# Attention and a gated feed-forward layer on one core: the first layer of eight chunks as seven Strassen products per pair of chunks, with streamed weight variants

## Chip, core and metric

The program runs on one core of one Trainium2 chip. The time is that of one execution on the device, in microseconds (us). Engines are named as in the profile: PE (TensorE, matmuls), PEld (its weight loads), DVE (VectorE), ACT (ScalarE), POOL (GpSimd) and SP (SyncE, which issues the DMAs here). Each engine works through its own list of instructions in order; semaphores make it wait for others.

## What is computed

```python
def _attn_ref(q, k, v, w_phi):                 # 8 batches, 8 heads, 576 tokens, 64 features
    def phi(x):
        proj = np.einsum('bhsd,df->bhsf', x, w_phi)
        proj = proj - np.max(np.abs(proj), axis=-1, keepdims=True)
        return np.concatenate([np.exp(proj), np.exp(-proj)], axis=-1)
    q_p, k_p = (phi(q), phi(k))
    kv = np.einsum('bhsf,bhsd->bhfd', k_p, v)
    z = np.sum(k_p, axis=2)
    num = np.einsum('bhsf,bhfd->bhsd', q_p, kv)
    den = np.einsum('bhsf,bhf->bhs', q_p, z)[..., None] + 1e-06
    return num / den
def _moe_ref(x, w_gate, w_val, w_out):         # x: 4608 tokens x 512, d_ff 1536
    g = x @ w_gate
    silu = g * (1.0 / (1.0 + np.exp(-g)))
    return silu * (x @ w_val) @ w_out
```

The attention's output, with the heads side by side, is the x of the second part. All of it is fp32; the weights come as 64-bit floats.

## The kernel before

**Tiles.** Attention works on 32 pairs of heads (pair i is batch i // 4, heads 2(i % 4) and the next). The feed-forward part works on twelve chunks of 384 tokens (`CH`), numbered 0 to 11 in the code, and on twelve slices f of 128 of the 1536 hidden features. The title's chunks 5 to 12 are 4 to 11 in the code.

**Split operands.** Most matmuls are made three times: each fp32 operand is split in a rounded high part (fp32r, by an ACT copy) and the rest (low, by a subtraction), and the product is hi*hi + hi*lo + lo*hi. All go through the helper `matmuls` (L274). So `first` (the gate and the value, `gv`) has 2 x 4 x 3 = 24 matmuls of 384 columns for a chunk and an f, and `second` (the second layer, into the banks `o`) nine of 512 columns. The high weights stay in SBUF (`w1_hi`, `w2_hi`); the low ones are stored in DRAM (`wlo_dram`) and loaded again for each chunk and f (`low_parts`, L618), 512 KB for the first layer and 256 KB for the second.

**Attention.** The first 8 pairs (`EARLY_PAIRS`) use plain fp32 matmuls and turn Q's projection with TensorE (L460); the other 24 split their operands and use VectorE's transposes. A pair projects K in five slots of 128 tokens (the last two overlap), takes the largest magnitude, makes both exponentials, sums `kv` and z in one matmul per slot, head and sign (20 of 128 columns, L411, with 64 columns of ones for z), projects Q, and makes numerators and denominators. The late pairs' exponentials are split by ACT (`qh`) and VectorE (`ql`, L534). The result is rounded and split into `xh`, `xl`, three sets of them, so attention can run at most that far ahead.

**Weights.** `weight_piece` turns 512 64-bit numbers per partition to fp32: a load, one ACT step, seven VectorE steps (L297 to L312), one ACT rounding, a store of the low part. There are 36 pieces, three for each f.

**Order.** The program is written as a list of steps with dependences, ranks and costs (`Plan`), and a list scheduler writes each engine's instructions in the order in which they could start by these costs. TensorE takes attention first (rank i) and feed-forward products behind it (rank 1000 and on); ACT, VectorE and SP take feed-forward steps first (`FIRST`). Chunks 0 to 2 run f by f while weights arrive (with 1 and 2 kept in `h_dram` for a second layer later); 3 to 11 follow one by one.

Of the kernel before, what the change touches and what calls it, by code (L numbers as in the profile page):

```python
# [17 lines left out]
P = 128  # L18
S = 576
# [25 lines left out]

# [11 lines left out]
class Plan:  # L57
# [3 lines left out]
    LAG = {"PE": 220, "ACT": 90, "DVE": 90, "SP": 2000}  # L61
# [120 lines left out]
def favor_attention_moe(ctx: ExitStack, tc: tile.TileContext, qT, kT, v, w_phi, wg, wv, wo, out):  # L182
# [7 lines left out]
    h_dram = tc.dram_tile([EARLY, NFT, P, CH], F32, name="h_dram")  # L190
# [56 lines left out]
    ps_kv = bank("kv")  # L247
    work = [bank(f"work{i}") for i in range(2)]
# [3 lines left out]
    wbd, wst = sb("wbd", [P, 2 * NF]), osb[1][:, :NF]  # L252
# [4 lines left out]
    for hi, lo, w in ((wbd_hi, wbd_lo, wbd), (wst_hi, wst_lo, wst)):  # L257
        nc.scalar.copy(hi, w)
        nc.vector.tensor_tensor(out=lo, in0=w, in1=hi, op=ALU.subtract)
    for h in range(2):  # L260
        nc.gpsimd.memset(vf[0][:, :, h, (1 - h) * D:(2 - h) * D], 1.0)
# [15 lines left out]
    weights_done = []  # L277
    w_ready, lo_stored, raw_free, wa_free = {}, {}, [None] * len(raw), [None] * len(wa)
    we_free = [None] * len(we)

    def weight_piece(f, a, rank):
# [10 lines left out]
        lo = w1_lo[f % LO_SETS][:, a].rearrange("p k f -> p (k f)") if a < 2 else w2_lo[f % LO_SETS]  # L292
# [16 lines left out]
        s6 = add("DVE", dve(n), lambda: vec.tensor_tensor(out=x, in0=x, in1=e, op=ALU.add), [s5], rank)  # L309
        we_free[u % len(we)] = s6  # L310
        s7 = add("ACT", act(n), lambda: nc.scalar.copy(hi, x), [s6], rank)
        s8 = add("DVE", dve(n), lambda: vec.tensor_tensor(out=lo, in0=x, in1=hi, op=ALU.subtract),  # L312
                 [s7, *(lo_user[a // 2][f - LO_SETS] if f >= LO_SETS else ())], rank)
# [8 lines left out]
    lo_user = ([], [])  # L322

# [4 lines left out]
    x_ready = {}  # L328
    early_done = []
# [3 lines left out]
    def attention(i, rank):  # L333
        b, pr = divmod(i, NPAIR)
        plan.early = early = i < EARLY_PAIRS
# [9 lines left out]
        k_in = add("SP", P * S * 4, lambda: nc.sync.dma_start(kin[j], kT[b, pr]), [last.get(("kin", i - 1))], rank)  # L345
# [11 lines left out]
        if early:  # L357
            k_ready = [k_in]
        else:
            k_hi = add("ACT", act(S), lambda: nc.scalar.copy(k_parts()[:, 0], kin[j]),  # L360
# [115 lines left out]
        else:  # L476
# [26 lines left out]
            def largest():  # L503
                vec.tensor_reduce(out=qm, in_=blocks(qe[j]), axis=AX.X, op=ALU.max, apply_absolute_value=True)
# [300 lines left out]
```

## Time and profile before

| What | Value |
|---|---|
| Timed runs, median of three (range) | 1305.03 us (1304.68 to 1305.92) |
| Span of the profiled execution, first to last instruction | 1304.0 us |
| Mean granted TensorE clock | 0.997 |
| First-layer matmuls (`gv`), 3456 of 384 columns, pieces of the chain | 45.3% of the span |
| Second-layer matmuls, 1296 of 512 columns (with others into the `o` banks) | 24.3% |
| `kv` matmuls of attention (L411) | 11.0% |
| Moved by DMA | 168.13 MB, mean 129 GB/s |

The profiled execution is one of the program; its time on the device beyond the span is not given, and the runs' median lies 1.0 us above the span. A group's row reads: line, engine, operation, output <- inputs, shapes, count | busy us, mean ns of one | idle time of the engine before them and what ended it. In the timeline a row has start, length, engine, line and operation, and x counts merged instructions.

### The profile page before, as it was taken

How to read it: one execution, taken by the hardware profiler on the slowest of the kernel's cores; microseconds unless marked ns; L12 is line 12 of the kernel's file. 1: busy time of each engine (PE TensorE's matmuls, PEld its weight loads, DVE VectorE, ACT ScalarE, POOL GpSimd, SP SyncE). 2: the span in 40 equal slices, each digit the busy share in tenths (PEclk: the TensorE clock that was granted, in tenths of full speed). 3: DMA queues.
4: the chain of work that ended last, by engine and by line, in shares of the span. 5: the costliest groups of instructions: out<-in, count | busy, mean ns of one | idle time of the engine just before them, and what ended most of it. 6: DMA issues, size and time to landing. Idle time of an engine off the chain costs nothing.

```text
span 1304.0 us, 19612 instructions
## 1 busy us (share of the span) xinstructions
PE 1281.7 (98%) x7554; PEld 1204.5 (92%) x7554; DVE 876.0 (67%) x1529; ACT 646.3 (50%) x1255; POOL 1.6 (0%) x9
## 2 busy tenths in 40 slices
PE   7999899999999999999999999999999999999998
PEld 6998899999778999999999999999999999999997
DVE  6997899997788767852777878732387786322222
ACT  5777433336676666631656665631365675221211
POOL 0000000000000000000000000000000000000000
PEclk9999999999999999999999999999999999999999
DMA  4343355553564443444443344354343443354443
GB/s 132 102 133 95 105 168 188 173 170 113 181 182 127 126 125 102 125 125 125 142 120 108 101 125 122 103 156 131 104 145 105 119 121 96 117 152 121 146 125 101
DMA packets 105564, 168.13 MB, mean 129 GB/s; under 512 B 46336, under 2 KB 52736, under 8 KB 105472
## 3 DMA queue, kind: packets, MB, share of 16 engines
q1 hardware_dynamic: 105152, 166.76, 43.1%
q8 instruction: 59, 0.97, 0.3%
q14 instruction: 33, 0.27, 0.1%
q10 hardware_dynamic: 320, 0.13, 0.0%
HBM read 143.26 MB, written 23.59 MB: 128 GB/s over the span
## 4 chain that ended last, share of the span: by engine, by line
PE 94%; DVE 2%; DMA 2%; ACT 1%; issue 1%; ACTq 0%; SPq 0%; DVEq 0%
PE gv L274 45%; PE o L274 24%; PE work L274 12%; PE kv L411 11%; DMA out_dram<-osb 1%; DMA w_lo<-wlo_dram 1%; PE o L460 1%; ACT osb L700 0%; DVE hl L677 0%; DVE km L387 0%; DVE qs L482 0%; DMA wbd<-in_w_phi_dram 0%; DVE kp L392 0%; DVE ql L534 0%; PE gv L751 0%
## 5 line engine op out<-in xcount | busy, mean ns | idle before, releaser
L274 PE MATMUL gv<-xh,w_hi 128*128 128x384 f32 x1152 | 389.4, 338 | 1.2 <-DVE th L653 1.2
L274 PE MATMUL gv<-xh,w_lo 128*128 128x384 f32 x1152 | 387.3, 336 | 0.0
L274 PE MATMUL gv<-xl,w_hi 128*128 128x384 f32 x1152 | 386.6, 336 | 0.0
L274 PEld LDWEIGHTS gv<-xh,w_hi 128*128 128x128 f32 x1152 | 216.7, 188 | 6.9 <-DVE th L653 1.9
L274 PEld LDWEIGHTS gv<-xl,w_hi 128*128 128x128 f32 x1152 | 216.7, 188 | 4.8
L274 PEld LDWEIGHTS gv<-xh,w_lo 128*128 128x128 f32 x1152 | 216.5, 188 | 0.0
L651 ACT ACTIVATE th<-gv 128x384 f32<-128x384 f32 x144 | 70.8, 492 | 265.8 <-PE gv L274 262.6
L653 DVE SCALAR_TENSOR_TENSOR th<-th,gv 128x384 f32<-128x384 f32 x144 | 78.9, 548 | 154.0 <-ACT th L651 153.5
L274 PE MATMUL o<-w_lo,hh 128*128 128x512 f32 x432 | 172.3, 399 | 1.0 <-DMA w_lo<-wlo_dram 0.8
L274 PE MATMUL o<-w_hi,hh 128*128 128x512 f32 x432 | 171.3, 396 | 2.0 <-ACT osb L700 1.8
L274 PE MATMUL o<-w_hi,hl 128*128 128x512 f32 x432 | 171.2, 396 | 0.0
L411 PE MATMUL kv<-vf,kp 128*128 128x128 f32 x1280 | 156.5, 275 | 0.0
L411 PEld LDWEIGHTS kv<-vf,kp 128*128 128x128 f32 x1280 | 153.0, 192 | 2.2 <-ACT kp L399 0.2
L676 ACT CAST hh<-th 128x384 fp32r<-128x384 f32 x144 | 73.7, 511 | 163.8 <-DVE th L656 148.6
L656 DVE TENSOR_TENSOR th<-th,gv 128x384 f32<-128x384 f32 x144 | 79.4, 551 | 67.2 <-PE gv L274 64.5
L399 ACT ACTIVATE kp<-kp 128x512 f32<-128x512 f32 (+1 forms) x192 | 105.8, 557 | 24.5 <-DVE kp L392 22.0
L568 DVE STREAM_TRANSPOSE qe<-den 128x576 f32<-128x576 f32 x32 | 24.9, 777 | 128.6 <-ACT den L561 128.6
L677 DVE TENSOR_TENSOR hl<-th,hh 128x384 fp32r<-128x384 f32 x144 | 79.2, 550 | 34.1 <-ACT hh L676 33.6
L274 PEld LDWEIGHTS o<-w_hi,hl 128*128 128x128 f32 x432 | 81.6, 189 | 19.1
L274 PEld LDWEIGHTS o<-w_lo,hh 128*128 128x128 f32 x432 | 81.5, 189 | 15.9 <-DMA w_lo<-wlo_dram 3.5
L274 PEld LDWEIGHTS o<-w_hi,hh 128*128 128x128 f32 x432 | 81.5, 189 | 15.3 <-ACT osb L700 2.6
L559 ACT COPY num<-work 64x288 f32<-64x288 f32 x103 | 40.5, 393 | 53.3 <-PE work L274 52.4
(103 smaller groups left out, 1762.7 us busy)
## 6 DMA issues: line engine op xcount, KB each, us to landing
w_lo<-wlo_dram SPq DMA_DIRECT2D x108, 512.0 KB, 3.6
w_lo<-wlo_dram SPq DMA_DIRECT2D x132, 256.0 KB, 3.1
kin<-in_kT_dram SPq DMA_DIRECT2D x32, 288.0 KB, 3.2
qin<-in_qT_dram SPq DMA_DIRECT2D x32, 288.0 KB, 2.9
wlo_dram<-w_lo SPq DMA_DIRECT2D x36, 256.0 KB, 2.3
out_dram<-osb SPq DMA_DIRECT2D x36, 256.0 KB, 3.2
vf<-in_v_dram SPq DMA_DIRECT2D x64, 128.0 KB, 3.1
shared<-in_wg_dram SPq DMA_DIRECT2D x12, 512.0 KB, 3.7
```

What stands on the lines that cost most here:

```text
L274: nc.tensor.matmul(o, l, r, start=a, stop=z)
L399: nc.scalar.activation(o, x, AF.Exp, scale=-1.0 if s else 1.0)
L411: nc.tensor.matmul(o, kp[buf][:, t - t0, h, s], vf[j][:, t, h], start=t == 0 and h + s == 0, stop=t == 4 and h + s == 2)
L460: nc.tensor.transpose(o[:, (h * w + t) * P:(h * w + t + 1) * P], y[:, 2 * t + h], ident)
L559: copied.append(add("ACT", act(SH), lambda key=key, ra=ra, c=c: nc.scalar.copy(num[ra, c], work[plan.bank[key]][ra, :SH]), [nu, free], rank))
L568: t0 = add("DVE", dve(S), lambda: vec.transpose(turned, den), [*copied, *done], rank)
L651: s1 = add("ACT", act(CH), lambda: nc.scalar.activation(t_, ps_gv[0][:, :CH], AF.Tanh, scale=0.5), [ends[0], th_free[j]], FIRST)
L653: s2 = add("DVE", dve(CH), lambda: nc.vector.scalar_tensor_tensor(out=t_, in0=t_, scalar=1.0, in1=ps_gv[0][:, :CH], op0=ALU.add, op1=ALU.m ...
L656: s3 = add("DVE", dve(CH), lambda: nc.vector.tensor_tensor(out=t_, in0=t_, in1=ps_gv[1][:, :CH], op=ALU.mult), [s2, ends[1]], FIRST)
L676: s4 = add("ACT", act(CH), lambda: nc.scalar.copy(hh[b], th[j]), [made, hid_free[b]], FIRST)
L677: s5 = add("DVE", dve(CH), lambda: nc.vector.tensor_tensor(out=hl[b], in0=th[j], in1=hh[b], op=ALU.subtract), [s4], FIRST)
```

## The change

**Products.** Chunks 4 to 11 are taken two at a time (c and c + 1). Their activations are split in two halves of the 512 input features, and gate and value play the two columns of a 2 x 2 block product. Strassen's form (Winograd's additions) makes it with seven products of 256 input features in place of eight. `operands` builds seven activation operands (three of them read as they are, four by four subtractions of VectorE) and splits each: seven ACT roundings and seven VectorE subtractions of 768 columns. `strassen` has, for each f, seven products of six matmuls (L965), three ACT copies out of a bank that goes on accumulating, three VectorE additions, two tanh and four multiplications behind them, of which the last is on GpSimd (L1036). Chunk c's second layer is done in three pieces (`piece`) among the products of the next f, with its `hl` by GpSimd; chunk c + 1's hidden values go to `h_dram`, and its second layer follows (`rest`).

**Weights.** Two of a piece's seven VectorE steps go to GpSimd (L332, L335). Three of the seven variants of the weights are copied from the raw high and low parts; four are sums, made by `sums` from a fp32 copy in DRAM (`w32_dram`) with GpSimd and one ACT rounding. All lie in `wv_dram`, and `strassen` streams each (256 KB) through a ring of twelve slots, which the second layer's low weights share. The high first-layer weights' place is then taken by the operands.

**Attention.** Twelve pairs are early instead of eight. K's last slot holds the last 64 tokens of both heads in one 128-column projection; `kv` has 16 matmuls of 65 columns and two of 130. `kv` takes a bank from the same three as the projections, and the products keep one of the three from chunk 4 on. The late `ql` are made by GpSimd. From chunk 3 on the output goes to DRAM (`x_dram`, L680) and is loaded again (`bring` for chunk 3, `operands` for the rest).

```diff
+EARLY_PAIRS = 12
+BANK_PAIRS = 8
+PLAIN = 4
+N_VAR = 7
...
-        s6 = add("DVE", dve(n), lambda: vec.tensor_tensor(out=x, in0=x, in1=e, op=ALU.add), [s5], rank)
+        s6 = add("POOL", pool2(n), lambda: nc.gpsimd.tensor_tensor(out=x, in0=x, in1=e, op=ALU.add), [s5], rank)
...
-        s8 = add("DVE", dve(n), lambda: vec.tensor_tensor(out=lo, in0=x, in1=hi, op=ALU.subtract),
-                 [s7, *(lo_user[a // 2][f - LO_SETS] if f >= LO_SETS else ())], rank)
+        s8 = add("POOL", pool2(n), lambda: nc.gpsimd.tensor_tensor(out=lo, in0=x, in1=hi, op=ALU.subtract),
+                 [s7, *(lo_user[a // 2][f - LOW_SETS[a // 2]] if f >= LOW_SETS[a // 2] else ()), *lo_copied.get(f - LO_SETS, ())], rank)
...
+        if a < 2:
+            wa_free[u % len(wa)] = stash[f, a] = add("SP", P * n * 4, lambda: nc.sync.dma_start(
+                w32_dram[f, :, a * DM:(a + 1) * DM], x), [s6, s8], rank)
...
+                        if both:
+                            nc.tensor.matmul(ps_kv()[:, s * 2 * VD:(s + 1) * 2 * VD], kp[buf][:, 0, 0, s],
+                                             vl.rearrange("p h d -> p (h d)"), start=False, stop=s == 1)
...
-                done += [g0, add("DVE", dve(2 * S), lambda k=k, part=part: vec.tensor_tensor(
+                done += [g0, add("POOL", pool2(2 * S), lambda k=k, part=part: nc.gpsimd.tensor_tensor(
                     out=flat(ql[k]), in0=flat(part), in1=flat(qh[k]), op=ALU.subtract), [g0, f1], rank)]
...
+            if c >= EARLY:
+                lo = add("SP", P * width * 4, lambda c=c, at=at, src=src, width=width: nc.sync.dma_start(
+                    x_dram[c - EARLY, :, pr, at:at + width], src), [t3], rank)
...
+    def stream(src, ready):
+        n = stream_n[0]
+        stream_n[0] += 1
+        stream_users[n] = []
+        older = stream_users[n - len(SLOTS_OF)] if n >= len(SLOTS_OF) else x_free[PLAIN - 1]
+        return n, add("SP", P * DM * 4, lambda: nc.sync.dma_start(stream_view(n).bitcast(F32), src),
+                      [*ready, *older], FIRST)
...
+        for f in range(NFT):
+            a, cc = gv(f, 0), gv(f, 1)
+            j1, s1 = unit
+            p2 = prod(f, 1, cc, True, [gv_read[(f + 1) % 2]])
+            g1 = plus(j1, cc, [s1, p2])
+            gv_read[(f + 1) % 2] = g1
+            t1, tg1 = gate(j1, g1)
+            p5 = prod(f, 4, zb, True, [third["free"]])
+            p6 = prod(f, 5, a, False, [s1])
+            j2, s2 = copy_out(a, [p6])
+            if f + 1 < NFT:
+                unit = begin_unit(f + 1)
+            else:
+                piece(0)
+            p7 = prod(f, 6, a, False, [s2])
+            j3, s3 = copy_out(a, [p7])
+            v2 = plus(j3, zb, [s3, p5])
...
+            p4 = prod(f, 3, a, False, [s3])
...
+            p3 = prod(f, 2, zb, False, [v2])
+            g2 = plus(j2, zb, [s2, p3])
...
-    for c in range(EARLY, NCH):
-        attend((c + 1) * CH)
-        for f in range(NFT):
-            j, h = first(c, f, low_parts(f, 0))
-            put_off(c, f, parts(j, h), low_parts(f, 1))
...
+    for c in range(PLAIN, NCH, 2):
+        attend((c + 2) * CH)
+        t = operands(c)
+        left = strassen(c, t, third, list(waiting))
+        waiting[:] = left
+        rest(c + 1)
```

**Where the instructions stand.** TensorE in the last chunks, before: `first` for one f, the gate's bank filled from end to end by twelve matmuls, then the value's (`xh`, `xl` the activations, `w1_hi`, `w1_lo` the weights).

```order
L274 MATMUL gv0_143<-xh2_99,w1_hi4_73 128x384
L274 MATMUL gv0_143<-xl2_102,w1_hi4_73 128x384
L274 MATMUL gv0_143<-xh2_99,w1_lo0_93 128x384
L274 MATMUL gv0_143<-xh2_99,w1_hi4_73 128x384
L274 MATMUL gv0_143<-xl2_102,w1_hi4_73 128x384
L274 MATMUL gv0_143<-xh2_99,w1_lo0_93 128x384
```

TensorE now, in the last pair of chunks, from p4 of one f to p7 of the next (`tb` the operands and some stream slots, `stream` the other slots, `work1` the third bank).

```order
L965 MATMUL gv0_139<-tb1_4439,tb3_4414 128x384 x6
L965 MATMUL work1_142<-tb1_4439,tb3_4414 128x384 x6
L296 MATMUL o2_138<-w2_hi7_83,hh1_127 128x512
L296 MATMUL o2_138<-stream_xl0_4396,hh1_127 128x512
L296 MATMUL o2_138<-w2_hi7_83,hl1_129 128x512
L965 MATMUL gv0_139<-tb0_4394,stream_xh0_4390 128x384 x6
L965 MATMUL work1_142<-tb2_4436,stream_xh0_4390 128x384 x6
L965 MATMUL gv1_140<-tb2_4436,stream_xl0_4396 128x384 x6
L965 MATMUL gv0_139<-tb0_4394,stream_xl0_4396 128x384 x6
L965 MATMUL gv1_140<-tb3_4414,stream_xl0_4396 128x384 x6
```

Each product has six matmuls; p6 and p7 go into the same bank (`gv1_140`) with one other product between them, and each waits until ACT has copied the bank.

VectorE in the weight stage, before: the end of one piece and the start of the next (`shared` the work tiles).

```order
L306 SCALAR_TENSOR_TENSOR shared_138<-shared_137,shared_138 128x512
L309 TENSOR_TENSOR shared_139<-shared_139,shared_138 128x512
L297 TENSOR_SCALAR shared_138<-shared_138 128x512
L299 TENSOR_SCALAR shared_138<-shared_138 128x512
L653 SCALAR_TENSOR_TENSOR th_128<-th_128,gv_143 128x384
L312 TENSOR_TENSOR w_lo_96<-shared_139,w_hi_90 128x512
```

GpSimd in the same stage now; before it had nothing there.

```order
L332 TENSOR_TENSOR shared3_135<-shared3_135,shared2_134 128x512
L335 TENSOR_TENSOR w1_lo1g_89<-shared3_135,w1_big1_73 128x512
L332 TENSOR_TENSOR shared3_135<-shared3_135,shared2_134 128x512
L335 TENSOR_TENSOR w1_lo1v_90<-shared3_135,w1_big1_73 128x512
L332 TENSOR_TENSOR shared3_135<-shared3_135,shared2_134 128x512
L335 TENSOR_TENSOR w2_lo2_93<-shared3_135,w2_hi5_81 128x512
```

L309 and L312 have become L332 and L335: six steps for each f, with an ACT rounding between the two of a piece.

SP's queue now, at the end of the products of a pair of chunks: stream loads, a store of hidden values that waits for GpSimd (L787), and attention's output (L680), in one order.

```order
L905 DMA stream_xh_4390<-wv_dram 128x512
L905 DMA tb_4414<-wv_dram 128x512
L787 DMA h_dram<-th_5212 128x384
L905 DMA tb_4414<-wv_dram 128x512
L680 DMA x_dram<-num 128x192
L680 DMA x_dram<-num 128x384
L420 DMA vf<-in_v_dram 128x4x64 x2
L423 DMA vl<-in_v_dram 64x64 x2
L905 DMA tb_4414<-wlo_dram 128x512
```

In the last chunks of before this queue held two loads of low weights for each f and the output's stores; a unit of products now loads eight tiles.

More of the change, by code (lines that the diff above doesn't have):

```diff
@@ L57 @@
 class Plan:
-    LAG = {"PE": 220, "ACT": 90, "DVE": 90, "SP": 2000}
+    LAG = {"PE": 220, "ACT": 90, "DVE": 90, "POOL": 90, "SP": 2000}
     BYTES = 250.0
@@ L246, in favor_attention_moe @@
     ps_gv = [bank(f"gv{a}") for a in range(2)]
-    ps_kv = bank("kv")
-    work = [bank(f"work{i}") for i in range(2)]
+    work = [bank(f"work{i}") for i in range(3)]
     make_identity(nc, ident)
-    wbd, wst = sb("wbd", [P, 2 * NF]), osb[1][:, :NF]
+    wb = sb("wb", [P, 3 * NF])
+    wbd, wst = wb[:, :2 * NF], wb[:, 2 * NF:]
     for h in range(2):
@@ L328, in favor_attention_moe, with staged, bring, tile @@
     x_ready = {}
+    staged_by, stages, t_made = {}, {}, {}
+    x_kept, x_used = {}, []
+    STAGE_TAGS = ("xh1", "xl1")
+    def staged(c):
+        n = (c - PLAIN) % N_STAGE
+        if n not in stages:
+            stages[n] = pool.tile([P, NK, CH], F32, name=f"stage{n}", tag=STAGE_TAGS[n])
+        return stages[n]
+    def bring():
+        xt = []
+        def tile():
+            if not xt:
+                xt.append(pool.tile([P, NK, CH], F32, name="x_kept", tag="xl1"))
+            return xt[0]
+        rank = EARLY_PAIRS - 0.5
+        load = add("SP", P * NK * CH * 4, lambda: nc.sync.dma_start(tile(), x_dram[0]),
+                   [*x_kept[EARLY], *x_free[1]], rank)
+        for pr in range(NPAIR):
+            hi = add("ACT", act(CH), lambda pr=pr: nc.scalar.copy(xh[0][:, pr], tile()[:, pr]), [load, *x_free[0]], rank)
+            lo = add("DVE", dve(CH), lambda pr=pr: nc.vector.tensor_tensor(
+                out=xl[0][:, pr], in0=tile()[:, pr], in1=xh[0][:, pr], op=ALU.subtract), [hi], rank)
+            x_ready[EARLY, pr] = [hi, lo]
+            x_used.extend([hi, lo])
+    turned_by = lambda: [last["qy", 3 * EARLY_PAIRS - n] for n in (1, 2)]
     early_done = []
@@ L404, in attention, with values @@
+            ksub = add("DVE", dve(n), centre, [kmax, last.get(("kp", 3 * i + g - 2))], rank, give=key)
+            e0 = add("ACT", act(n), lambda f=exponential: f(0), [ksub], rank)
+            e1 = add("ACT", act(n), lambda f=exponential: f(1), [e0], rank)
             last["km", 3 * i + g] = ksub
-            def values(t0=t0, t1=t1, buf=buf, g=g):
+            def values(t0=t0, t1=t1, buf=buf, both=both):
                 for t in range(t0, t1):
-                    for h in range(2):
-                        for s in range(2):
-                            o = ps_kv[:, (2 * h + s) * P:(2 * h + s + 1) * P]
-                            nc.tensor.matmul(o, kp[buf][:, t - t0, h, s], vf[j][:, t, h],
-                                             start=t == 0 and h + s == 0, stop=t == 4 and h + s == 2)
```

441 lines of the change are left out of this document (341 added, 100 removed).

## The prediction

> **What bounds the kernel now.** I read the page's shares first, then its chain, then a table of windows, to see whether any stage has another limit.
>
> ```profile
> PE 1281.7 (98%) x7554; PEld 1204.5 (92%) x7554; DVE 876.0 (67%) x1529; ACT 646.3 (50%) x1255; POOL 1.6 (0%) x9
> PE 94%; DVE 2%; DMA 2%; ACT 1%; issue 1%; ACTq 0%; SPq 0%; DVEq 0%
> 0.00:130.00 130.00, 121.60 (x740) 109.31 (x741) 108.72 (x204) 90.39 (x201) 1.62 (x9) 1.00 0.41 116
> 130.00:330.00 200.00, 193.89 (x1116) 187.21 (x1114) 177.52 (x333) 85.18 (x156) 0.00 (x0) 0.99 0.48 156
> 330.00:400.00 70.00, 67.87 (x385) 57.41 (x386) 55.44 (x89) 50.18 (x93) 0.00 (x0) 0.98 0.60 175
> 400.00:1100.00 700.00, 699.36 (x4270) 664.95 (x4269) 477.06 (x803) 379.00 (x725) 0.00 (x0) 1.00 0.41 120
> 1100.00:1304.00 204.00, 198.99 (x1050) 185.65 (x1048) 57.23 (x101) 41.53 (x83) 0.00 (x0) 1.00 0.42 127
> ...
> PE gv L751 <- ACT wbd_hi L258: 7.5, 1, 7.5
> ```
>
> The columns of the windows are PE, PEld, DVE, ACT and POOL busy, the clock, the DMA share and GB/s; the last row is one of the view of waits. TensorE ends the chain for 94% of the span, and idles 22.3 us in all: 16.6 before 400 us (7.5 of it the start, by that row), 0.6 in the next 700 us, 5.0 in the tail. VectorE is at 84 to 89% up to 330 us and is the only other engine near a limit; later it has slack. So the first question is how much TensorE work goes, and the second which new waits a full TensorE meets. TensorE's busy time overlaps itself, so I price matmuls by their pace, start to start.
>
> **Paces.**
>
> ```profile
> 600.78 4.19 PE gv L274 x24
> 276.00 12.51 PE gv L274 x72
> 290.61 12.51 PE gv L274 x72
> 43.16 3.73 PE L411 MATMUL kv<-vf,kp 128*128 128x128 f32 x32
> 49.77 1.05 PE L411 MATMUL kv<-vf,kp 128*128 128x128 f32 x8
> 46.73 1.04 PE L460 MATMUL o<-ident,qy 128*128 128x128 f32 x8
> 47.60 0.60 PE L274 MATMUL work<-wbd,qin 128*128 128x256 f32 x2
> 51.83 1.89 PE L274 MATMUL o<-wbd,qin 128*128 128x256 f32 x8
> 53.56 0.65 PE L274 MATMUL o<-qe,kvs 128*128 128x288 f32 x2
> 54.04 0.65 PE L274 MATMUL o<-qx,kvs 128*128 128x288 f32 x2
> ...
> 398.10 0.29 PE L274 MATMUL work<-ql,kvh 128*128 128x288 f32 x1
> ...
> 399.29 0.30 PE L274 MATMUL work<-ql,kvh 128*128 128x288 f32 x1
> ...
> 404.81 0.27 PE L274 MATMUL work<-wbd_hi,ks 128*128 128x256 f32 x1
> ...
> 405.28 0.28 PE L274 MATMUL work<-wbd_lo,ks 128*128 128x256 f32 x1
> ```
>
> The first three are pieces of the chain (start, length): a first-layer matmul of 384 columns takes 4.19/24 = 0.1746 us; in the weight stage one f repeats every 290.61 - 276.00 = 14.61 us, so its nine second-layer matmuls take 14.61 - 12.51 = 2.10 (0.233 each). The rest are rows of the timeline. Plain fp32 matmuls have two records each, except the transposes. kv: (3.73 - 1.05)/24 = 0.112 per record. A transpose (47.60 - 46.73)/8 = 0.109. fp32, 256 columns: (53.56 - 51.83)/4 = 0.432 per matmul; 288 columns: 54.04 - 53.56 = 0.485, which is 0.842 ns per column and record. Split matmuls of 288 columns: (399.29 - 398.10)/9 = 0.132; of 256: (405.28 - 404.81)/4 = 0.118.
>
> **TensorE work, part by part** (counts from the program's order).
> - First layer: 3456 matmuls become 1152 in chunks 1 to 4 and 2016 in the products. 288 x 0.1746 = **-50.3**. Their width and number per bank are as before, so I keep the pace.
> - kv: 640 matmuls of 128 columns become 512 of 65 and 64 of 130. The trace has no matmul of 65 columns. If a record stays at 0.112 whatever its width, only the count falls: 128 records, **-14.3**. If it goes by columns, 65 x 0.842 = 0.055, and the sum is -72. I take 0.112: at 128 columns, columns alone would give 0.108, so the row lies at or above that line, and the nearest row is the safe end; -72 stays as a rival. The Trainium skill (TensorE: Matmul & The Clock Gate, section LDWEIGHTS) gives a weight load as columns/1.2 ns, 107 ns for 128 whatever the moving width, and its fast load is not for fp32; by that the term would be about -19. The 0.112 above agrees, though no run so far shows a narrow moving side.
> - K's last slot: one 128-column projection for both heads. Together with four pairs more on the fp32 path: 40 x 0.432 + 360 x 0.118 = 59.8 before; 48 x 0.432 + 240 x 0.118 = 49.1 now, plus 12 fp32 and 60 split matmuls of 128 columns, which lie between half of the 256-column price (6.1) and the whole (12.3). Between -4.6 and +1.6; I take **-3**.
> - Q of these four pairs, fp32 with transposes for split: 40 x 0.432 + 80 x 0.109 + 192 x 0.132 = 51.3 becomes 60 x 0.432 + 120 x 0.109 + 160 x 0.132 = 60.1: **+8.8**. Numerators: 64 x 0.485 + 576 x 0.132 = 107 becomes 96 x 0.485 + 480 x 0.132 = 110: **+3**.
> - The second layer stays at 1296.
>
> Sum: -50.3 - 14.3 - 3 + 8.8 + 3 = **-56**, so 1304 - 56 = 1248 with the idle time of before.
>
> **The other engines.**
>
> ```profile
> L309 DVE TENSOR_TENSOR shared<-shared,shared 128x512 f32<-128x512 f32 x36 | 24.8, 690 | 0.9
> L312 DVE TENSOR_TENSOR w_lo<-shared,w_hi 128x512 fp32r<-128x512 f32 x36 | 24.3, 684 | 0.0
> L297 DVE TENSOR_SCALAR shared<-shared 128x512 f32<-128x512 f32 x36 | 15.1, 419 | 0.0
> L534 DVE TENSOR_TENSOR ql<-qe,qh 128x1152 fp32r<-128x1152 f32 x24 | 32.4, 1352 | 1.7 <-ACT qh L531 1.6
> L677 DVE TENSOR_TENSOR hl<-th,hh 128x384 fp32r<-128x384 f32 x144 | 79.2, 550 | 34.1 <-ACT hh L676 33.6
> L520 ACT ACTIVATE qe<-qx 128x1152 f32<-128x1152 f32 x24 | 28.0, 1166 | 30.9 <-DVE qx L518 30.9
> L261 POOL MEMSET vf<- 128x320 f32 x2 | 0.7, 367 | 0.0
> masks.py:199 POOL TENSOR_SCALAR_AFFINE_SELECT ident<-ident 128x128 f32<-128x128 f32 x1 | 0.3, 293 | 0.0
> L795 POOL MEMSET const-float32-1.0<- 128x1 f32 x1 | 0.1, 103 | 0.0
> ```
>
> VectorE loses two steps of every weight piece, 36 x (0.690 + 0.684) = 49 us, where it was fullest; also the ql of all late pairs. That can return part of the 9.1 us that TensorE idles before 400 us beside the start: I take -5, bounds 0 and -9.1.
>
> GpSimd gets these steps. The trace has no two-input operation of it. Writing alone costs (0.367 - 0.103)/319 = 0.83 ns an element, one read and a write (0.293 - 0.103)/127 = 1.5; one more read at 0.8 gives my estimate of 2.3: 1.3 us for 512 elements, 2.75 for 1152, 1.0 for 384. Bounds: 0.83 ns and twice the estimate. In the weight stage six such steps an f are 7.7 us of the 14.61 that TensorE needs; behind a late GpSimd step stand ACT's rounding, SP's store and, in SP's order, the next weight load. A late pair has two ql, 5.5 us where VectorE took 2.7; numerators, in TensorE's fixed order, wait for them.
>
> ```profile
> 1210.65 0.33 PE L274 MATMUL gv<-xh,w_lo 128*128 128x384 f32 x1
> ...
> 1211.02 0.49 ACT L651 ACTIVATE th<-gv 128x384 f32<-128x384 f32 x1 [3.05 <-PE gv L274]
> ...
> 1211.55 0.55 DVE L653 SCALAR_TENSOR_TENSOR th<-th,gv 128x384 f32<-128x384 f32 x1 [2.98 <-ACT th L651]
> ```
>
> These are the gate's steps of before: ACT starts 0.37 us after the last matmul of a bank starts, takes 0.49, and the next engine starts 0.04 later, 0.90 in all. In a product unit (42 matmuls and nine of the second layer, 42 x 0.1746 + 2.10 = 9.43 us) every accumulation that reuses a bank waits for a copy by ACT. The tightest is p7 behind p6: the next unit's first product lies between, so p7 could start 7 x 0.1746 = 1.22 us after the last matmul of p6 started, and the copy is through at 0.90. ACT has six such steps in 9.43 us and VectorE six at 0.55. So it fits with 0.3 us of room, and one 1.17 us exponential of attention (L520) ahead of it on ACT takes more than that; all that stands behind p7 in TensorE's queue would wait too.
>
> I take +14 for all new waits, under a third of what the second rival would cost; bounds 0 and that rival's 47. Net +9: **1257 of span**. The timed runs have a median of 1305.03 for a span of 1304.0, 1.0 more: **1258**.
>
> **Rivals.**
>
> *GpSimd and VectorE hold each other up.* If steps that read two SBUF operands, or VectorE's fast tensor_scalars (0.42 for 512), never run beside a GpSimd step, an f of the weight stage has 3 x (3 x 0.42 + 2 x 0.69) + 0.55 = 8.5 us on VectorE and 7.7 on GpSimd: 16.2 against 14.61, +1.6 x 12 = 19. Later a ql waits on average half of a 1.35 us step: 20 pairs x 2 x 0.7 = 28. Sum 47: 1248 + 47, **1295**. Against it: much of the attention work of VectorE reads PSUM, and its bank-freeing steps do. The Trainium skill (SBUF — State Buffer, section Who interferes with whom) states this as a rule: such pairs share an exclusive lock and the second blocks fully. No row here shows GpSimd reading beside VectorE.
>
> *Slower: GpSimd becomes the bound.* Six steps an f fit in 14.61 us up to 2.43 us each. At 2.6 for 512 elements (twice my estimate): 12 x (15.6 - 14.61) = 12, and two ql of 5.85 at 3.1 over estimate, half of it exposed: 20 x 3.1 = 62. **1323**; it decides from about 2.45 us a step.
>
> *The streams bind.*
>
> ```profile
> 380.00:390.00 10.00, 9.29 (x43) 7.09 (x42) 9.69 (x18) 5.56 (x9) 0.00 (x0) 1.00 0.75 229
> w_lo<-wlo_dram SPq DMA_DIRECT2D x132, 256.0 KB, 3.1
> ```
>
> A unit loads eight tiles of 256 KB and stores 192 KB, 2.29 MB in 9.43 us: 243 GB/s, more than the 229 of the busiest 10 us here. There the engines were at 0.75, so 305 is in reach, and twelve stream slots of 3.1 us loads cover half a unit more. If only 225 is delivered, a unit takes 10.2: +0.77 x 48 = 37, **1295**; at 220 the change does nothing.
>
> *kv by columns*: 58 less, **1200**.
>
> **Chances.** Forecast 0.55 (own range 1240 to 1275), lock 0.18, GpSimd bound 0.12, streams 0.08, kv by columns 0.07. The range leaves out the last and the slow one: **1232 to 1306**. About 0.2% is what a measurement of this kernel tells from no change. Faster: all but GpSimd and part of the streams, 0.84; same 0.03; slower 0.13.
>
> **What would show it.** Gains: 288 fewer gv matmuls at 0.175; kv records at 0.11. Waits: TensorE idle for ACT copies between p6 and p7, or for ql; GpSimd steps well over 1.3 us for 512 elements, or VectorE's steps longer than 0.69 beside them; a period over 14.61 us in the weight stage; loads that land later than 10 us. Wrong would be a pace of the products over 0.18, or idle TensorE over 40 us behind GpSimd.

## The result, and the profile after

| Kernel | Median | Range | Ratio to before, 95% interval |
|---|---|---|---|
| before | 1305.03 us | 1304.68 to 1305.92 | |
| after | 1368.7 us | 1367.14 to 1370.91 | 1.0488 (1.0469 to 1.0507), slower |

The forecast was 1258 (1232 to 1306). The profiled execution of after has a span of 1366.7 us. First the engines' busy time from the page of after, four of the windows that were shown of before, and the 50 us in which the products start:

```profile
PE 1264.1 (92%) x7136; PEld 1148.8 (84%) x7136; DVE 919.1 (67%) x1440; ACT 709.4 (52%) x1407; POOL 391.3 (29%) x280
0.00:130.00 130.00, 121.76 (x743) 108.91 (x743) 106.41 (x197) 93.04 (x217) 20.34 (x26) 1.00 0.48 141
130.00:330.00 200.00, 196.43 (x1149) 184.11 (x1149) 167.10 (x273) 95.46 (x196) 65.01 (x48) 1.00 0.62 196
330.00:400.00 70.00, 60.92 (x315) 54.11 (x314) 52.12 (x78) 34.76 (x63) 29.96 (x19) 0.96 0.70 230
400.00:1100.00 700.00, 637.16 (x3698) 579.61 (x3698) 499.54 (x736) 401.62 (x767) 233.31 (x147) 0.97 0.66 208
500.00:550.00 50.00, 31.71 (x167) 28.52 (x167) 39.05 (x48) 25.43 (x44) 14.48 (x8) 0.76 0.66 214
```

TensorE idles 1366.7 - 1264.1 = 102.6 us, where it idled 22.3. From 400 to 1100 us it idled 0.6 and now 62.8, and 18 of these lie between 500 and 550, where the products start. VectorE gave away work, took over the operands' subtractions, and is busy for 919 us, more than the 876 of before. The view of the chain can't be compared: the shares by engine that it gives for after add up to some 40% of the span only. Who ends TensorE's waits (total, times, longest; a selection):

```profile
PE work L296 <- ACT qx L587: 16.6, 3, 14.6
PE o L296 <- DVE hl L801: 12.5, 9, 4.0
PE gv L296 <- DVE th L777: 9.7, 9, 3.6
PE work L296 <- DVE kp L469: 9.3, 8, 2.7
PE gv L965 <- DMA tb<-wv_dram: 7.0, 3, 3.4
PE gv L965 <- DMA stream_w_lo<-wv_dram: 6.1, 4, 4.3
PE gv L965 <- DMA stream_xl<-wv_dram: 5.2, 7, 1.2
PE o L296 <- POOL hl L801: 2.0, 3, 0.8
```

The view of waits names VectorE, ACT and streams, and GpSimd for 2.0 us only. What GpSimd does stands in the durations. Groups of after (before the bar busy us and mean ns):

```profile
L801 DVE TENSOR_TENSOR hl<-th,hh 128x384 fp32r<-128x384 f32 x96 | 74.2, 780 | 65.0 <-ACT hh L799 63.1 <-DMA th<-h_dram 1.5 <-issue 0.2
L574 DVE TENSOR_TENSOR qs<-qin,qs 64x576 fp32r<-64x576 f32 x40 | 53.0, 1324 | 6.5 <-ACT qs L572 5.6
L986 DVE TENSOR_TENSOR th<-th,work 128x384 f32<-128x384 f32 x96 | 52.7, 549 | 106.5 <-ACT th L983 91.2 <-PE work L965 15.0
L627 POOL TENSOR_TENSOR ql<-qe,qh 128x1152 fp32r<-128x1152 f32 x20 | 56.9, 2844 | 161.7 <-ACT qh L624 152.7 <-DVE kp L469 9.0
L801 POOL TENSOR_TENSOR hl<-th,hh 128x384 fp32r<-128x384 f32 x48 | 52.5, 1094 | 373.4 <-ACT hh L799 373.3
L332 POOL TENSOR_TENSOR shared<-shared,shared 128x512 f32<-128x512 f32 x36 | 48.7, 1353 | 156.8 <-DVE shared L329 156.8
```

GpSimd's steps are near the estimates (1.35 us for 512 columns, 2.84 for 1152, 1.09 for 384). VectorE's steps with two SBUF inputs grew: hl took 550 ns in before (that row is in the prediction), and 780 now; qs took 753 and now 1324; one with a PSUM input (L986) still takes 549. A single case, from the timeline (start, length; in brackets the wait before):

```profile
499.20 2.37 POOL L866 TENSOR_TENSOR s<-s,shi 128x1024 fp32r<-128x1024 f32 x1 [2.29 <-ACT shi L865]
500.01 2.17 DVE L667 TENSOR_TENSOR num<-num,den 128x576 f32<-128x576 f32 x1
502.10 0.28 DVE L469 TENSOR_TENSOR kp<-work,km 128x128 f32<-128x128 f32 x1
502.44 0.40 PE L296 MATMUL work<-qs,wst_hi 128*128 128x288 f32 x1 [0.87 <-DVE kp L469]
```

VectorE's num step took 756 ns on average in before. Here it takes 2.17 us and ends 0.6 us after GpSimd's step, as if it had begun only shortly before that step's end. L469, which reads PSUM and has no part in it, stands behind it in VectorE's queue, and TensorE waits for L469.

**The sum of TensorE's work.** For each matmul I took the time from its start to the start of the next, less the median of this time for its kind (line, tiles and shape), where that was over 60 ns, and added these up: 27 us in before, 144 in after. Spans less these sums: 1304.0 - 27.3 = 1276.7 and 1366.7 - 144.4 = 1222.3. So the work fell by 54 us, and 117 us of waits came. The split is an estimate: with the kind taken from the later matmul, or from both, the work falls by 63 or by 47, and the waits grow by 126 or by 109.

### The profile page after: what moved, and what is told of

It reads as the page before. It is cut to its first block, busy times and chain, and to the rows that moved or that the text cites. A ratio compares the mean times of both kernels' runs of the same rounds, so it can differ in the third digit from the quotient of the medians.

```text
span 1366.7 us, 20915 instructions
## 1 busy us (share of the span) xinstructions
PE 1264.1 (92%) x7136; PEld 1148.8 (84%) x7136; DVE 919.1 (67%) x1440; ACT 709.4 (52%) x1407; POOL 391.3 (29%) x280
## 5 line engine op out<-in xcount | busy, mean ns | idle before, releaser
L296 PE MATMUL gv<-xh,w_big 128*128 128x384 f32 x384 | 134.8, 351 | 10.0 <-DVE th L777 9.7
L296 PE MATMUL gv<-xl,w_big 128*128 128x384 f32 x384 | 130.0, 339 | 0.0
L986 DVE TENSOR_TENSOR th<-th,work 128x384 f32<-128x384 f32 x96 | 52.7, 549 | 106.5 <-ACT th L983 91.2
L983 ACT COPY th<-gv 128x384 f32<-128x384 f32 x144 | 68.6, 478 | 96.5 <-PE gv L965 88.6
L489 PEld LDWEIGHTS work<-vf,kp 128*128 128x128 f32 x800 | 93.8, 192 | 2.6 <-ACT den L654 1.1
L991 DVE SCALAR_TENSOR_TENSOR th<-th,th 128x384 f32<-128x384 f32 x96 | 69.0, 720 | 38.5 <-ACT th L990 38.2
L489 PE MATMUL work<-vf,kp 128*128 128x65 f32 x800 | 92.9, 273 | 0.9 <-ACT den L654 0.9
L332 POOL TENSOR_TENSOR shared<-shared,shared 128x512 f32<-128x512 f32 x36 | 48.7, 1353 | 156.8 <-DVE shared L329 156.8
L296 PEld LDWEIGHTS gv<-xh,w_big 128*128 128x128 f32 x384 | 73.1, 190 | 15.1 <-DVE th L777 13.4
L965 PE MATMUL gv<-tb,stream_xh 128*128 128x384 f32 x408 | 82.6, 339 | 2.6 <-DMA stream_xh<-wv_dram 2.5
L965 PE MATMUL gv<-tb,stream_xl 128*128 128x384 f32 x384 | 77.0, 340 | 5.5 <-DMA stream_xl<-wv_dram 5.2
L965 PEld LDWEIGHTS gv<-tb,stream_xh 128*128 128x128 f32 x408 | 71.0, 188 | 7.1 <-DVE th L991 4.0
```

The costliest lines, as they stand in the source:

```text
L296: nc.tensor.matmul(o, l, r, start=a, stop=z)
L332: s6 = add("POOL", pool2(n), lambda: nc.gpsimd.tensor_tensor(out=x, in0=x, in1=e, op=ALU.add), [s5], rank)
L489: nc.tensor.matmul(ps_kv()[:, (2 * s + h) * VD:(2 * s + h + 1) * VD], kp[buf][:, t - t0, h, s], vf[:, t, h], start=t == 0 and h + s == 0, ...
L965: nc.tensor.matmul(o(), l, r, start=begin and k + m == 0, stop=k + m == 3, skip_group_check=True)
L983: return j, add("ACT", act(CH), lambda: nc.scalar.copy(th(j), src()), [*after, th_free[j]], FIRST)
L986: return add("DVE", dve(CH), lambda: vec.tensor_tensor(out=th(j), in0=th(j), in1=src(), op=ALU.add), after, FIRST)
```

## The experiments

The last column is the sum just described. Runs 1 to 4, 5 to 8, 9 to 12 and 13 to 16 shared a chip each with runs of before; ratios are to those.

| Run | Kernel | Median us | Ratio (95%) | Waits us |
|---|---|---|---|---|
| 2 | after, all GpSimd steps given back to VectorE | 1314.4 | 1.0073 (1.0053 to 1.0093) | 90 |
| 3 | after, only the late steps given back | 1321.7 | 1.0125 (1.0110 to 1.0140) | 99 |
| 4 | after, only the weight stage's steps given back | 1364.9 | 1.0466 (1.0446 to 1.0485) | 140 |
| 5 | after, ql and sums given back | 1319.1 | 1.0109 (1.0094 to 1.0124) | 98 |
| 6 | 3, streams halved | 1295.5 | 0.9928 (0.9914 to 0.9943) | 75 |
| 7 | 3, operands behind | 1312.3 | 1.0056 (1.0038 to 1.0074) | 89 |
| 8 | before, two work banks | 1318.3 | 1.0101 (1.0084 to 1.0118) | 39 |
| 9 | 7, own tiles for w_lo | 1299.5 | 0.9947 (0.9932 to 0.9962) | 73 |
| 10 | 7, bank taken late | 1315.3 | 1.0080 (1.0061 to 1.0100) | 89 |
| 11 | 7, both | 1297.2 | 0.9930 (0.9915 to 0.9945) | 70 |
| 12 | before, ql on GpSimd | 1345.1 | 1.0302 (1.0287 to 1.0318) | 66 |
| 13 | after, ql alone given back | 1331.9 | 1.0205 (1.0190 to 1.0220) | 108 |
| 14 | after, own tiles alone | 1349.2 | 1.0333 (1.0306 to 1.0360) | 120 |
| 15 | 11, hl and h2 on GpSimd | 1294.7 | 0.9920 (0.9905 to 0.9935) | 74 |
| 16 | 15, operands further behind | 1293.0 | 0.9899 (0.9882 to 0.9915) | 70 |

Span less waits is 1220 to 1223 us in all thirteen kernels built on after, and 1277 to 1278 in the two built on before. Only the waits differ. After each edit the planner puts the engines' instructions in order anew, so a difference between two kernels holds what the new order does, too; no run keeps the order fixed.

### Do the two engines hold each other? (run 1)

A kernel of its own: twelve steps of 512 columns on each engine, alone and side by side, and six GpSimd steps of 1152 columns.

> A kernel that computes nothing of the reference: loops of single steps of 512 columns on VectorE and GpSimd, first alone, then side by side. Lock: a VectorE step with two SBUF inputs (0.69 us alone) and a fast tensor_scalar beside GpSimd's two-input steps (1.3 us) take turns with them, so 12 pairs last 12 x (0.69 + 1.3) = 24 us; VectorE steps with one PSUM input, transposes and reductions keep their time and the phase lasts 12 x 1.3 = 16 us. Bandwidth rival: both slow down by a part, 12 pairs last 17 to 20 us, and the steps with one input get longer as well.

Groups from windows of this kernel: first VectorE alone (nine steps in a row, from the timeline), then with two SBUF inputs beside GpSimd's 512 and 1152 columns, with one PSUM input, as a tensor_scalar, a transpose and a reduction, and last GpSimd beside these:

```profile
13.29 6.51 DVE L48 TENSOR_TENSOR dc<-da,db 128x512 f32<-128x512 f32 x9
L48 DVE TENSOR_TENSOR dc<-da,db 128x512 f32<-128x512 f32 x8 | 12.1, 1513 | 0.2
L63 POOL TENSOR_TENSOR pc<-pa,pb 128x512 f32<-128x512 f32 x7 | 11.3, 1609 | 0.6
L48 DVE TENSOR_TENSOR dc<-da,db 128x512 f32<-128x512 f32 x7 | 18.6, 2652 | 0.2
L66 POOL TENSOR_TENSOR ps__72<-pq,pr 128x1152 f32<-128x1152 f32 x6 | 17.7, 2944 | 2.6 <-DVE pq L44 2.2
L51 DVE TENSOR_TENSOR dc<-da,bk 128x512 f32<-128x512 f32 x6 | 4.1, 687 | 0.2
L54 DVE TENSOR_SCALAR dc<-da 128x512 f32<-128x512 f32 x11 | 14.1, 1280 | 0.3
L57 DVE STREAM_TRANSPOSE dc<-da 128x512 f32<-128x512 f32 x11 | 7.8, 708 | 0.3
L60 DVE TENSOR_REDUCE dc<-da 128x16 f32<-128x512 f32 x12 | 8.2, 682 | 0.3
L63 POOL TENSOR_TENSOR pc<-pa,pb 128x512 f32<-128x512 f32 x36 | 45.4, 1262 | 24.5 <-DVE pq L44 21.9
```

The lock is there, and one engine pays most: VectorE's step goes from 0.69 (0.73 start to start, first row) to 1.51 us beside 512 columns and to 2.65 beside 1152, its tensor_scalar from 0.42 (before's row) to 1.28. Each of these means has one step in it that was not held; by the timeline the held ones take 1.63, 2.98 and 1.37 us. GpSimd's goes from 1.26 (last row, beside transposes, reductions and ACT copies) to 1.61. With one PSUM input, in transposes and reductions VectorE keeps its time. Twelve pairs take 12 x (1.609 + 0.6/7) = 20 us, not the 24 of strict turns. It looks as if the end of one step lies over the start of the next; a pair takes 1.67 us where 0.69 + 1.26 = 1.95 would be strict turns. 20 us is the bandwidth rival's total, but under it the transposes and reductions would have grown as well. The Trainium skill (SBUF — State Buffer, section Who interferes with whom) states this division, and that who issues first holds the ports for the whole instruction. These rows agree with the division; of the turns they show somewhat less than the whole.

### What the holds cost, and where (runs 2, 3, 4, 5, 13)

Each of the five changed kernels gives some steps back, in this manner (here ql):

```diff
-done += [g0, add("POOL", pool2(2 * S), lambda k=k, part=part: nc.gpsimd.tensor_tensor(
+done += [g0, add("DVE", dve(2 * S), lambda k=k, part=part: nc.vector.tensor_tensor(
```

> The changed kernel with every GpSimd step given to VectorE. Lock theory: VectorE's busy time is 919 - 118 (what its two-input steps gained beside GpSimd) + 190 (the steps it takes over) = about 990 us; the waits for VectorE and ACT chains (about 60 us of TensorE's stalls) and most of the 18 us at a low clock go, the waits for streams (27 us) stay: 1290 to 1310 us. Rival, streams and the chain of banks: at most 10 us better, 1358 or more. Rival, VectorE was relieved by the change and now is too full: slower than 1369.

> Only the steps after the weight stage (ql, weight sums, hl, h2) are given to VectorE; the weight stage keeps its GpSimd steps. Lock theory: about the time of the kernel with everything on VectorE, within 8 us, since TensorE's waits lie behind 350 us: 1290 to 1315 us. Rival, streams: 1358 or more.

> Only the weight stage's 72 GpSimd steps are given back to VectorE. Lock theory: the first 350 us change by less than 8 us, as VectorE's two-input steps there got as much longer as the removed ones were short; the late waits stay: 1360 to 1375 us. Rival, the weight stage is where the time went: 1345 or less.

> The changed kernel with ql and the weight sums on VectorE; hl and h2 of the product units (96 steps of 384 columns) and the weight stage stay on GpSimd. Lock theory, price by the time that GpSimd holds VectorE: ql and sums are 40 x 2.85 + 12 x 6.0 = 186 of the 291 us of late GpSimd work, so 30 of the 47 us return: about 1338 us. If a long hold costs more than several short ones, 1320 to 1330. Rival, hl and h2 stand in the cycle of banks and cost most: 1355 or more.

> The changed kernel with ql alone on VectorE; weight sums, hl, h2 and the weight stage stay on GpSimd. If the 40 ql steps (2.85 us each, beside attention's own chains) make the price, most of the 49 us that ql and sums cost together return: 1322 to 1330 us. If the 60 steps of the sums (1.0 to 2.4 us) cost their share of GpSimd's time, 72 of 186, about 1338 us.

Runs 2 and 3 lie 4 and 7 us above the range of the lock theory, and 44 and 36 us below the streams' rival, which falls as the main cause. Run 4 can't be told from after, but runs 2 and 3, which differ in the weight stage's steps alone, lie 7 us apart with intervals that don't meet. So the holds of the weight stage cost little, not nothing. The two windows of run 4 up to 330 us, with these steps back on VectorE:

```profile
0.00:130.00 130.00, 121.19 (x730) 107.21 (x731) 110.37 (x210) 92.62 (x215) 1.20 (x12) 1.00 0.49 141
130.00:330.00 200.00, 199.87 (x1160) 189.33 (x1160) 170.64 (x323) 92.53 (x192) 0.00 (x0) 1.00 0.64 206
```

TensorE idles 8.9 us here and 11.8 in after; in runs 2 and 3 it is 8.5 and 11.4. VectorE is busy for 281.0 us with the 72 steps and for 273.5 without them.

In run 2, with GpSimd idle, VectorE's groups have their old durations again:

```profile
L801 DVE TENSOR_TENSOR hl<-th,hh 128x384 fp32r<-128x384 f32 x144 | 79.3, 551 | 51.0 <-ACT hh L799 44.9
L574 DVE TENSOR_TENSOR qs<-qin,qs 64x576 fp32r<-64x576 f32 x40 | 30.1, 753 | 2.3 <-ACT qs L572 1.4
```

Run 5 takes back as much as run 3 (their intervals overlap), so hl and h2 in the product units cost nothing that can be measured on GpSimd, though they hold steps too (L991, two SBUF inputs, takes 633 ns in run 5 and 551 in run 2). ql and the sums cost 49 us. Run 13, between the two ranges given for it, divides these: 37 for ql, the other 13 for the sums. By the holding time run 5 was expected at 1338; but the 105 us of hl and h2 are free, the sums cost 13 for their 72 us, ql 37 for 117. So the price does not go by holding time. Whether the length of a hold decides, or what stands beside it, these runs don't separate: beside ql VectorE does the next pair's qs and ks (two SBUF inputs), with the PSUM-freeing steps of the pair queued behind. Nor do they separate a second path: ql itself takes 2.8 to 3.0 us on GpSimd, where before's took 1.35 on VectorE, and ACT waits for it ten times in after, 10.2 us in all. TensorE's own waits never name ql.

### The same edit in the kernel before (run 12)

The same line as in the diff above, from VectorE to GpSimd, in before; the planner is told GpSimd's cost.

> The kernel before with one change, its 48 ql steps on GpSimd. Lock theory: each holds VectorE's two-input steps for up to 2.9 us, and some 20 to 45 us are added, 1325 to 1350 us; hl and the ks, qs and num steps beside them show 1 to 3 us. Rival, in the old order VectorE's slack hides the holds: within 5 us of 1305.

Two groups of VectorE and TensorE's largest wait in this run:

```profile
L486 DVE TENSOR_TENSOR qs<-qin,qs 64x576 fp32r<-64x576 f32 x48 | 108.6, 2263 | 1.4
L681 DVE TENSOR_TENSOR hl<-th,hh 128x384 fp32r<-128x384 f32 x144 | 96.9, 674 | 35.1 <-ACT hh L680 34.4
PE work L278 <- DVE qs L486: 19.3, 14, 3.3
```

The same qs group in before:

```profile
L482 DVE TENSOR_TENSOR qs<-qin,qs 64x576 fp32r<-64x576 f32 x48 | 36.1, 753 | 1.2
```

It costs 40 us for 48 ql, with no product, stream or third accumulator in the program. VectorE was spared 65 us (two groups of ql like the prediction's of 32.4) and got 72 more in qs alone. ks (795 ns, 751 in before) and num (752 and 756) hardly changed, where 1 to 3 us had been expected.

### Streams: the rate or the slot? (runs 6, 9, 14)

Run 6 loads half of each streamed weight variant:

```diff
-hi, lo = a[:, k * NF:(k + 1) * NF], a[:, (2 + k) * NF:(3 + k) * NF]
+hi = lo = a[:, k * NF:(k + 1) * NF]
...
-got[f, v] = stream(wv_dram[f, v], wv_stored[f, v])
+got[f, v] = stream(wv_dram[f, v, :, :2 * NF], wv_stored[f, v], 2 * NF)
```

> The kernel with the late steps on VectorE, and only the high half of each streamed weight variant is loaded (128 KB instead of 256); the matmuls use the high half in the place of the low one too, so the low part of these weights is left out of the sums. Nothing else changes. Streams theory: the waits for streamed tiles (27 us in all) go for the most part: 1295 to 1303 us. Rival, the waits lie in the change of stage at 500 us and in the order of the engines: 1315 or more.

26 us, as the streams theory had it; but fewer bytes also land sooner, so it leaves open why they were late. Runs 9 and 14 leave the bytes and change who holds a slot. There are eleven ring slots for seven loads a unit then, and two tiles for the eighth, 13 in place of 12, so one tile more is part of the edit (lines of run 14):

```diff
-STREAM = [("xh0", 3), ("xl0", 3), ("w1_lo0", 2), ("w1_lo1", 1), ("w1_big3", 3)]
+STREAM = [("xh0", 3), ("xl0", 3), ("w1_lo0", 2), ("w1_big3", 3)]
...
+        if own:
+            k = own_n[0] % 2
+            own_n[0] += 1
+            older, own_users[k] = own_users[k], users[n]
+            return n, lambda: own_tile(k), [add("SP", P * DM * 4, lambda: nc.sync.dma_start(
+                own_tile(k).bitcast(F32), wlo_dram[f, :, 2 * DM:]), [lo_stored[f, 2], *older], FIRST)]
...
-pend.append((c, f, parts(t1, h1, True), low_parts(f, 1)))
+pend.append((c, f, parts(t1, h1, True), low_parts(f, 1, own=True)))
```

> As the run with the operands behind, but the streamed low part of the second layer has two tiles of its own while products run, and no longer a slot of the ring of twelve: held from its load to the end of the next unit, it makes SP wait for its slot's next load, and every load behind stands too. Theory: it is the ring and not the rate of the DMA engines that makes TensorE wait for streams; at the end of the program a unit takes 9.5 us and not 10.3, and 12 to 20 us go: 1292 to 1300 us. Rival, 222 GB/s is what the DMA engines give with these transfers: the unit stays at 10.3 and the time within 4 us of 1312.3.

> The changed kernel with all its GpSimd steps, and only the streamed low part of the second layer in tiles of its own. If the ring and GpSimd's holds are separate causes, the same 12.8 us go as without the holds: 1354 to 1358 us, and a unit at the end takes 9.5 us. If the holds hide the ring's waits: 1363 or more.

Starts of the unit's last step (h2) in the last pair of chunks, first in after, then in run 9, and the window of these twelve units in each (PE, PEld, DVE, ACT, POOL busy, clock, DMA share, GB/s):

```profile
1236.61 1.02 POOL L1036 TENSOR_TENSOR th<-th,th 128x384 f32<-128x384 f32 x1 [0.68 <-DVE th L991]
1246.41 1.02 POOL L1036 TENSOR_TENSOR th<-th,th 128x384 f32<-128x384 f32 x1 [0.63 <-DVE th L991]
1256.74 1.02 POOL L1036 TENSOR_TENSOR th<-th,th 128x384 f32<-128x384 f32 x1 [0.62 <-DVE th L991]
1226.00:1337.00 111.00, 105.59 (x553) 97.09 (x552) 36.72 (x67) 33.47 (x67) 22.44 (x23) 1.00 0.75 235
```

```profile
1199.01 0.56 DVE L1049 TENSOR_TENSOR th<-th,th 128x384 f32<-128x384 f32 x1
1208.43 0.56 DVE L1049 TENSOR_TENSOR th<-th,th 128x384 f32<-128x384 f32 x1
1160.00:1264.00 104.00, 102.67 (x551) 97.03 (x550) 46.44 (x88) 33.02 (x66) 0.00 (x0) 1.00 0.79 249
```

With the slots mended seven of the eleven units in run 9 take 9.42 or 9.43 us, which is 42 x 0.1746 + 2.10 to the digit, and their mean is 9.51 (9.49 in run 14); in after the two shown are 9.80 and 10.33, and the mean is 10.08. The engines then move 249 GB/s, where loads were late at 235. So it was the ring and not the rate. One case in after: the second layer's last reader of a slot, the next load into this slot, and the product that needs it.

```profile
1244.60 0.40 PE L296 MATMUL o<-stream_xl,hh 128*128 128x512 f32 x1
1245.03 0.33 SPq L905 DMA_DIRECT2D stream_xl<-wv_dram  x1
1249.01 0.59 PE L965 MATMUL gv<-tb,stream_xl 128*128 128x384 f32 x2 [0.63 <-DMA stream_xl<-wv_dram]
```

The second layer's low part keeps its slot to the end of the next unit. The load that takes over this slot goes out 4.0 us before TensorE needs it and lands after 3.85; the unit's other loads go out 12 to 15 us ahead. It is this one load that is late: by their semaphores 18 of TensorE's 20 stream waits in after, 15.7 of 20.8 us, are for a load that a second-layer matmul released. That SP stands for this slot with every load behind it, as expected for run 9, did not show: in the planned order the other loads stand ahead, and in this window SP waits for a second-layer matmul once, 0.4 us.

12.8 us go in run 9, 19.5 in run 14, where 12.8 had been expected: the ring costs as much or more beside the holds, so the two causes are separate. What halving the bytes gives beyond the ring wasn't separated.

### Where the products start (runs 7, 8, 10, 11, 16)

TensorE's longest wait in run 3, last column, begins at 505 us:

```profile
PE work L296 <- DVE kp L469: 20.3, 6, 13.3
```

There VectorE makes the products' operands in one piece, ahead of attention's steps. The 14.6 us under `ACT qx` in after lie at the same place, from 522 to 536 us, while VectorE makes the operands.

```diff
-vec, rank = nc.vector, FIRST + 0.5
+vec, rank = nc.vector, NPAIR * (((c + 2) * CH + S - 1) // S) + 0.5
```

Run 16 has 2.5 in the place of 0.5. Run 8 is before with

```diff
+        if c == EARLY + 1:
+            add("PE", 1, lambda: None, x_free[EARLY], -2.0, take="third")
```

and runs 10 and 11 take the bank behind a late step of the second layer (`near`) and give it back after a pair of chunks:

```diff
-    third = {"free": add("PE", 1, lambda: None, x_free[PLAIN - 1], -2.0, take="third")}
+    third = {"free": None}
...
+        third["free"] = add("PE", 1, lambda: None, [third["free"], *near], -2.0, take="third")
         left = strassen(c, t, third, list(waiting))
...
-            g2 = plus(j2, zb, [s2, p3])
+            g2 = plus(j2, zb, [s2, p3], "third" if f == NFT - 1 else None)
```

> The kernel with the late steps on VectorE, and the eleven VectorE and seven ACT steps that make the product operands stand behind the attention steps of the next pair in the planner's order, not ahead of all. Theory: the idle 13.7 us of TensorE at 504 us is their lump of 12 us on VectorE, with attention's steps behind it and an attention matmul ahead of ready second-layer matmuls in TensorE's order: 1303 to 1311 us. Rival, what lacks there is a bank or the data: within 5 us of 1321.7.

> The kernel before, with one of its three work banks taken away for good when the first layer of chunk 3 ends, as the third accumulator of the products takes it. Bank theory: attention's projections then wait for one another, and 15 us or more are added, 1320 us or more. Rival, two banks do: within 4 us of 1305.

> As the run with the operands behind, but the third accumulator takes its bank only some 6 us before a pair of chunks starts its products, and gives it back at their end. Bank theory: the 50 us of second layer between the first layer of chunk 3 and the first product have three banks for attention again, and the three later stretches of 25 us too: 5 to 13 us go, 1299 to 1307 us. Rival, the lump at 505 us comes from VectorE's queue alone: within 3 us of 1312.3.

> Both of these edits. If they are apart in place and cause, their gains add: the sum of the two, within 4 us. If they are two sides of one wait, the better of the two.

> The same, with the operands' steps behind two more attention pairs in the planner's order. In the run with ring and bank mended they are still one lump of 13 us on VectorE at 502 us, ahead of the pair's kvl, and TensorE stands 11.2 us behind it. Theory of the lump: 8 to 11 us go against the run before it, 1281 to 1288 us. Rival, VectorE is full there whatever the order: within 3 us of that run.

Run 7 gains 9 us, 1 less than the least expected, and not from the stretch that it was made for: TensorE still waits 13.4 us there, and 10.8 in run 11, which has the same rank. The gain is spread over 600 to 1050 us, where the operands of the later chunks are made. The bank is worth 13 us in the old order (run 8, a little under the 15 expected), and nothing when given back in the new one (run 10 against 7, run 11 against 9: intervals overlap). Run 16 breaks the piece up; its longest wait after the start is 4.4 us. The first row is the long wait of run 11, the other two are this wait of run 16 and its window at this place:

```profile
PE work L296 <- DVE kvl L515: 11.2, 2, 10.8
```

```profile
PE work L296 <- DVE kp L469: 15.9, 9, 4.4
490.00:535.00 45.00, 35.73 (x210) 31.59 (x209) 41.37 (x68) 31.28 (x56) 0.00 (x0) 0.92 0.82 264
```

The time is within the interval of run 15, so the theory of the lump falls: VectorE is busy for 41.4 of these 45 us, and it seems that whichever step goes first, another is late.

### All that helped (run 15)

> All edits that helped, with hl and h2 on GpSimd: ql and sums on VectorE, operands behind, tiles of its own for the low part, the bank late. If hl and h2 (1.1 us each) cost nothing on GpSimd, as the run with ql and sums alone on VectorE tells (2.5 us below the one with all late steps there): 1291 to 1297 us. If they cost their share: 1305 or more.

It came out at 1294.7. Runs 15 and 16 lie 0.8 and 1.0% below before, with intervals that leave out 1, and 5.4 and 5.5% below after. Both still have the weight stage's steps on GpSimd.

## Why the prediction failed, by its steps

- **TensorE's work, -56: right.** Measured 1276.7 - 1222.3 = 54, or 47 to 63 by the other ways of counting. The products keep 0.1746 (the units of run 9). kv stays at the record's price whatever its width, and so the rival by columns fell; two rows of after's timeline, 32 records of 65 columns and the next matmul, give (551.77 - 548.28)/32 = 0.109:

```profile
548.28 3.68 PE L489 MATMUL work<-vf,kp 128*128 128x65 f32 x32
551.77 0.38 PE L296 MATMUL work<-qs,wst_hi 128*128 128x288 f32 x1
```

- **VectorE's relief before 400 us, -5: this step failed as well.** Up to 330 us TensorE idles 11.8 us and not 14.5, by the windows, but the steps given to GpSimd are not the reason: with them back on VectorE it idles 8.9 (run 4). The 49 us taken off VectorE freed 7.5, because the steps that stayed got longer (L320, a tensor_scalar, 708 ns where before's L297 took 419). From 330 to 400 us, where the first ql steps and sums run, TensorE loses 7.0 more than before.
- **GpSimd's durations: right**, and the rival in which GpSimd becomes the bound fell with them.
- **The bank cycle of a unit, room of 0.3 us at p6 and p7: right.** Seven units of run 9 take the 9.43 us that the matmuls' paces give, so no bank makes them wait.
- **"+14 for all new waits, bounds 0 and 47": this is the step that put the time outside the range.** It was taken as a third of the rival of the lock (the first in the list, though the prediction calls it the second), with no row for GpSimd reading beside VectorE. It was 117. Taken apart by the runs: 49 for ql and sums on GpSimd, 13 to 20 for the slots of the ring, about 9 for the operands ahead of attention, and some 42 that the best kernel still has above before's 27. Part of these lies at the change of stage around 500 us, where VectorE is full, and some 3 in the weight stage; the cause of the rest is open. Whether the granted clock, 0.76 in 500 to 550 against 1.00 before, is a cause there or follows the idle stretches, no run tells apart.
- **The rival of the lock (47, chance 0.18) had the mechanism, and its total by luck.** It put 19 on the weight stage, where the difference is 3 us of TensorE's idle time (7 of the whole between runs 2 and 3), and 28 on ql, with GpSimd waiting half of a VectorE step. It is mostly VectorE that waits, for up to a whole GpSimd step; ql costs 37, and the sums, which it left out, 13. The argument against it, that bank-freeing steps read PSUM, missed that they stand in the same queue behind steps that read SBUF twice. Run 12 shows that this price needs nothing else of the change.
- **The rival of the streams** had the right size for a unit (10.2 us; 10.08 measured) for the wrong reason: it took a rate of 225 GB/s as the limit. Its total of 37 was 13 to 20. "Twelve slots cover half a unit more" counted slots, not how long each is held.
- **"Idle TensorE over 40 us behind GpSimd"** as the sign of a failure would never have shown: the view of waits has 2.0 us of it. A step that is held counts as busy on its own engine (hl, 780 ns for 550).
- **Small sums.** The 1.0 us from span to time is 2.0 for after (1368.7 and 1366.7), and the -19 that the prediction gives for kv beside its own term comes to -20 by the figures that stand there. Neither matters beside 117.

## What to carry to other kernels

Before work goes to GpSimd, list the VectorE steps that will run beside it by their inputs: here those with two SBUF inputs, and the tensor_scalars, waited for most of the GpSimd step, and so did all that was queued behind them, whatever it read. In this kernel 96 steps of 1.1 us in the product units cost nothing that could be measured, and 40 of 2.9 us beside attention cost 37 us. When loads into a ring are late, look at which slot is held longest before blaming the rate: a unit came out at 10.1 us at 235 GB/s and at 9.5 at 249, with the same bytes. Subtract the sum of matmul paces from the span; if that agrees with the forecast, the error lies in the waits, and edits that give back one thing at a time can be set against them. Here they found some 75 of 117 us.

## What the runs showed of the hardware that had not been expected

- Of two steps that hold each other, VectorE's lost most: 0.69 to 1.51 us beside GpSimd's 512 columns, where GpSimd's went from 1.26 to 1.61 (run 1).
- GpSimd's step with one SBUF input (a tensor_scalar of 512 columns) takes longer than its two-input add (by run 1's timeline 1.49 us alone, the add 1.26) and holds VectorE less. Run 1, VectorE with two SBUF inputs beside it (804 ns on average):

```profile
L69 POOL TENSOR_SCALAR pc<-pa 128x512 f32<-128x512 f32 x7 | 11.6, 1660 | 1.6 <-DVE pq L45 1.1
L48 DVE TENSOR_TENSOR dc<-da,db 128x512 f32<-128x512 f32 x10 | 8.0, 804 | 0.2
```
